# Routing's choice over two iterations, its subtraction on GpSimd, and the fullest expert found in five VectorE operations

## The chip, the cores and the metric

One core of a Trainium2 chip runs the whole kernel as one program. The metric is the device time of one execution in microseconds (us). TensorE (PE) does the matrix products and writes them to PSUM; VectorE (DVE), ScalarE (ACT) and GpSimd (POOL) work on tiles of 128 partitions; SyncE (SP) issues most of the DMAs, and GpSimd issues the indirect ones. Each engine executes its own instructions in order and waits for the others through semaphores.

## The reference

Attention with random features is followed by a mixture of experts with one expert for each token.

```python
h = x @ omega.T - sum(x * x) / 2          # q and k, scaled; batch 8, heads 8, sequence 576, dim 64, features 128
phi = exp(h - max(h)) / sqrt(m)
num = phi(q) @ (phi(k).T @ v);  den = phi(q) @ sum(phi(k)) + 1e-6
x = (num / den) as 4608 tokens x 512
logits = (x / |x|) @ (emb / |emb|).T / tau     # 8 experts
expert_idx = argmax(logits);  gate_w = softmax(logits)[expert_idx]
for e in range(8):
    out[mask_e] = gate_w * (relu(x[mask_e] @ w1[e]) @ w2[e])    # 512 x 1024 x 512
```

## The kernel before

The 4608 tokens are 36 tiles of 128. The first stage is one loop over iterations i from 0 to 42 (END = NTILE + LAG): iteration i projects the keys of tile i and the queries of tile i - 6, and finishes the numerators of tile i - 7. The order of the instructions on all five engines is written out by hand. The order in an iteration is: two projections on TensorE (`proj`, L328, psum tiles pjk and pjq, 64 x 128 x 128 each), the turning of the query features (`qtr`, L404, into nub), maxima on VectorE (`maxima`, L332, tiles nmk and nmq), copies of the turned features (`qcopy`, L409, tile qp, one half on ScalarE and one on VectorE), exponentials on ScalarE (`feats`, L339), the numerators (`num`, L428, into nub), the sums over keys (`kvmm`, L354, kva), and the division on VectorE (`num_out`, L440 to L446), which also leaves each token's eight logits (lg). The psum tile nub is used in turn by L404 and L428, so the next turning waits for the division. After every fifth or ninth tile the sums are closed and turned (L376 to L394), which lengthens that iteration.

Every three tiles make a group (G = 3, groups 0 to 11). The generator `routed(g)` does the routing of a group in steps, and the loop hangs each step on a place in a later iteration, with dictionaries `mid`, `after`, `then` and `ends` that are emptied at fixed points of an iteration (`go`). For a group whose steps begin in iteration b these are:

- step 0, iteration b, at its end: the logits are summed over the heads on GpSimd (L460).
- step 1, iteration b + 1, at `then`: the maximum over the experts (L470) and its subtraction (L471) on VectorE, and three copies of the result into the token rows on GpSimd (L473).
- step 2, iteration b + 1, at `ends`: the first expert that reaches the maximum, in three VectorE operations (L476 to L478, tile sel). From iteration 36 on (group 9 and later) it stands at `mid` of b + 2.
- step 3, iteration b + 2, at `after`: the counting matmuls (L484, L486) that give each token its place among its expert's tokens.
- steps 4 and 5, iteration b + 2, at `ends`: the places on VectorE (L492, L493) and GpSimd (L495, L460), and the first of three casts (L505) and indirect scatters of the rows to DRAM (L507) from GpSimd.
- steps 6 and 7, iterations b + 3 and b + 4, at `ends`: the second and third scatter.

Iteration b + 3 is the b of the next group, and there step 0 of that group is emitted ahead of `go(ends)`. After group 5 (GPICK) `pick_first` finds the fullest expert (L518 to L523) and, one iteration later, `first_known` computes from it (L527 to L532) the addresses (firsti) with which SyncE loads that expert's weights during the loop, and isf and keyc, which are read after the loop. From iteration 28 on these weights are loaded (`first_weights`) and split into two parts each by ScalarE (L545) and GpSimd (L548, and `second_pieces`, L556 and L557, in 16 pieces that the dictionaries `ahead` and `behind` hang on iterations 30 to 41). Iterations 37 to 42 also fill TensorE with the first rows' expert products (`first_steps`, tiles fs_a and fs_o).

The second stage starts at about 235 us: 36 further steps of 128 rows each through an expert's two matrices, in three products each for precision (`products`, L240, psum tiles pa and nu).

## Time and profile before

| | |
|---|---|
| runs of the kernel, us | 638.98, 636.65, 635.66; median 636.65 |
| the profiled execution, us | 639.68 |
| its span from first to last instruction, us | 637.8 |
| mean granted TensorE clock in it | 0.998 of full speed (2.4 GHz) |
| TensorE matmul busy | 620.9 us (97%) |
| VectorE busy | 488.7 us (77%), 953 instructions |
| ScalarE busy | 413.8 us (65%) |
| GpSimd busy | 322.6 us (51%), 420 instructions |

Busy shares are means over stages with different limits. Matmuls are pipelined and their ends are modelled, so a TensorE that is always busy need not be at its peak. The chain of work that ended last is followed back from the last instruction, at each step to what released it; it tells which engine set the pace at each time. "Issue" in it is time in which an engine waited for nothing that the profile shows.

### The profile page before, as it was taken

To read this page: it belongs to the slowest core of one execution; us is meant where nothing else is said; L and a number is where in the kernel's file an instruction comes from. 1 tells how busy PE (TensorE), PEld (TensorE's weight loads), DVE (VectorE), ACT (ScalarE), POOL (GpSimd) and SP (SyncE) were. 2 spreads that over 40 slices of the span, in tenths; PEclk is the share of its full clock that TensorE was granted. 3 is DMA by queue.
4 is the path that set the end of the run, shared out by engine and by line. 5 is a ranking of instruction groups with operands and counts; after the bars stand their busy time and mean duration, and the time that the engine had idled before them with its cause. 6 is when DMAs were issued, how large, how long until landed. Compare 5 with 4: busy or idle time off the path is not lost.

```text
span 637.8 us, 18619 instructions
## 1 busy us (share of the span) xinstructions
PE 620.9 (97%) x6339; PEld 531.7 (83%) x6340; DVE 488.7 (77%) x953; ACT 413.8 (65%) x1071; POOL 322.6 (51%) x420
## 2 busy tenths in 40 slices
PE   8999999999988999999999999999999999999996
PEld 7999999999877787888888888888888888888885
DVE  4799899898778745797688777878777878788652
ACT  5899899889886417664556555656555656565630
POOL 2014333336888744447355646464655555464623
PEclk9999999999999999999999999999999999999999
DMA  7646666668752277878988888898878897979741
GB/s 255 185 153 218 198 209 216 205 226 287 267 194 69 100 251 268 248 203 223 209 238 201 240 208 208 221 234 216 220 203 209 238 231 193 230 218 208 211 117 45
DMA packets 142362, 131.89 MB, mean 207 GB/s; under 512 B 106742, under 2 KB 106870, under 8 KB 142272
## 3 DMA queue, kind: packets, MB, share of 16 engines
q1 hardware_dynamic: 135808, 110.04, 63.8%
q0 software_dynamic: 6320, 20.38, 8.2%
q8 instruction: 57, 0.93, 0.6%
q10 hardware_dynamic: 144, 0.26, 0.2%
q14 instruction: 33, 0.27, 0.1%
HBM read 83.78 MB, written 21.97 MB: 166 GB/s over the span
## 4 chain that ended last, share of the span: by engine, by line
PE 86%; DVE 6%; ACT 3%; issue 3%; DMA 1%; SPq 1%; POOL 0%; POOLq 0%; DVEq 0%; ACTq 0%
PE pa L240 31%; PE nu L240 29%; PE pjk L328 5%; PE nub L428 5%; PE kva L354 5%; PE pjq L328 3%; PE nub L404 2%; PE fs_o L240 2%; ACT ftq L339 1%; ACT ftk L339 1%; PE fs_a L240 1%; DVE qp L409 1%; DVE nmk L332 1%; DVE nmq L332 1%; DMA emb_sb<-emb 1%
## 5 line engine op out<-in xcount | busy, mean ns | idle before, releaser
L240 PE MATMUL nu<-w2h,hh 128*128 (+1 forms) x288 | 112.4, 390 | 0.0
L240 PE MATMUL nu<-w2h,hl 128*128 (+1 forms) x288 | 112.1, 389 | 0.0
L240 PE MATMUL nu<-w2l,hh 128*128 (+1 forms) x288 | 112.0, 389 | 0.0
L240 PE MATMUL pa<-w1h,xh 128*128 (+1 forms) x280 | 109.6, 391 | 0.1
L240 PE MATMUL pa<-w1h,xl 128*128 (+1 forms) x280 | 109.2, 390 | 0.0
L240 PE MATMUL pa<-w1l,xh 128*128 (+1 forms) x280 | 109.0, 389 | 0.0
L953 ACT ACTIVATE pl<-pa 128x512 uint16<-128x512 uint16 x68 | 39.8, 590 | 82.2 <-DMA t<-pl 58.0
L949 DVE TENSOR_REDUCE wd<-t 128x1024 uint16<-128x1024 uint16 (+1 forms) x70 | 90.1, 1292 | 2.2 <-DMA t<-pl 2.1
L339 ACT ACTIVATE ftk<-pjk,nmk 128x128 f32<-128x128 f32 x288 | 85.3, 433 | 5.8 <-DVE nmk L332 5.5
L339 ACT ACTIVATE ftq<-pjq,nmq 128x128 f32<-128x128 f32 x288 | 80.1, 434 | 7.6 <-DVE nmq L332 7.1
L206 POOL TENSOR_TENSOR w1l<-raww,w1h 128x1024 f32 x33 | 80.2, 2432 | 9.3 <-DVE w1h L205 8.3
L949 DVE TENSOR_REDUCE pl<-pa 128x512 uint16<-128x512 uint16 x68 | 46.5, 686 | 47.2 <-ACT pl L953 46.8
L206 POOL TENSOR_TENSOR w2l<-raww,w2h 128x1024 f32 x33 | 79.6, 2411 | 3.8 <-DVE w2h L205 3.8
L328 PE MATMUL pjk<-om,kt 64*128 64x128 f32 x576 | 75.9, 283 | 0.2 <-DVE om L624 0.2
L328 PE MATMUL pjq<-om,qt 64*128 64x128 f32 x576 | 75.6, 283 | 0.3 <-ACT ftk L339 0.2
L993 ACT ACTIVATE hh<-wd 128x1024 fp32r<-128x1024 f32 x33 | 35.0, 1061 | 60.1 <-DVE wd L949 54.2
L328 PEld LDWEIGHTS pjk<-om,kt 64*128 64x128 f32 x576 | 64.5, 188 | 2.8 <-DVE om L624 0.5
L270 POOL DMA_INDIRECT y<-xgp x20 | 22.6, 1132 | 84.2 <-DVE xgp L247 75.6
L328 PEld LDWEIGHTS pjq<-om,qt 64*128 64x128 f32 x576 | 63.9, 188 | 1.2 <-ACT ftk L339 0.7
L240 PEld LDWEIGHTS nu<-w2h,hl 128*128 128x128 f32 x288 | 54.1, 188 | 11.3
L240 PEld LDWEIGHTS nu<-w2h,hh 128*128 128x128 f32 x288 | 54.0, 188 | 11.2 <-issue 0.2
L240 PEld LDWEIGHTS nu<-w2l,hh 128*128 128x128 f32 x288 | 54.0, 188 | 11.2
(313 smaller groups left out, 1262.8 us busy)
## 6 DMA issues: line engine op xcount, KB each, us to landing
raww<-w1q SPq DMA_DIRECT2D x38, 512.0 KB
raww<-w2q SPq DMA_DIRECT2D x38, 512.0 KB
qt<-qT SPq DMA_DIRECT2D x36, 256.0 KB
kt<-kT SPq DMA_DIRECT2D x35, 256.0 KB
xgp<-xs SPq DMA_DIRECT2D x20, 260.5 KB
xg<-xs SPq DMA_DIRECT2D x18, 260.5 KB
rf<-w1q SPq DMA_DIRECT2D x4, 512.0 KB
rf<-w2q SPq DMA_DIRECT2D x4, 512.0 KB
```

The source lines that it names most:

```text
L206: il = nc.gpsimd.tensor_tensor(at(l, dp), raw, at(h, dp).bitcast(F32), op=ALU.subtract)
L240: done.append(nc.tensor.matmul(dst, x[:, c * P : (c + 1) * P], ws.rearrange("p o f -> p (o f)"), start=(begin and i == 0 and k == 0), stop ...
L270: w = nc.gpsimd.indirect_dma_start(out=out, out_offset=bass.IndirectOffsetOnAxis(ap=xg[:, PAY - 1 : PAY].bitcast(I32), axis=0), in_=xg[:, ...
L328: nc.tensor.matmul(st["pj" + w, i, a][:, c, :], st[w, i][r, c, :], om[r, :], start=True, stop=True)
L332: nc.vector.tensor_reduce(nm, st["pj" + which, i, a], axis=AX.X, op=ALU.max, negate=True)
L339: nc.scalar.activation(ft[:, h, :], pj[:, h, :], AF.Exp, bias=nm[:, h : h + 1])
L354: nc.tensor.matmul(acc[c : c + 64, h, :], ft[:, h, c : c + 64], vt[:, 2 * h + a, :], start=begin and h == 0, stop=u == 4 + 4 * b and h == 3,)
L404: nc.tensor.transpose(nu[z][:, j * 64 : j * 64 + 64], st["fq", i, j // 4][r, j % 4, :], ident[r, r])
L428: nc.tensor.matmul(pn[a][z * 64 : z * 64 + 64, h, :], st["qp", i, z][:, 4 * a + h, :], kvs[sb, int(b)][:, h, a * HW : (a + 1) * HW], start ...
L949: nc.vector.tensor_reduce(to, src.unsqueeze(2), axis=AX.X, op=ALU.max)
L953: nc.scalar.activation(planes[1][:, o : o + 512], halved(src)[:, :, 1], AF.Copy)
L993: nc.scalar.activation(hh, wd[:, 0:F], AF.Relu)
```

## The change

Five things change. The subtraction of the maximum goes from VectorE to GpSimd for groups 0 to 6 (GSUB = 7). The last of the three choosing operations (L478) is emitted in the step of the counting matmuls, ahead of them, for groups 0 to 8 (GSEL = 9). The second scatter of a group hangs on a new place, `soon`, in iteration b + 3, which is emptied ahead of step 0 of the next group. The fullest expert is found with a compare and a product in one operation, and the addresses come from one operation over a small table (placei) that GpSimd fills before the loop, in place of five; isf and keyc are computed by three operations of GpSimd in place of two of VectorE, and the tile `first` is gone. One piece of weight splitting in iteration 40 is emitted at `after` and not at the iteration's end.

```diff
 G = 3
 REG = N + P
 GPICK = 5
+GSUB, GSEL = 7, 9
 DUM = E * REG
 ROWS = DUM + P
 RS = 576
...
     isf = const.tile([P, E], F32, name="isf")
     tabi = const.tile([5, NSTEP], I32, name="tabi")
     runi = const.tile([P, E], I32, name="runi")
-    first = const.tile([P, 1], F32, name="first")
     firsti = const.tile([P, NPRE + 2], I32, name="firsti")
     xgp = [const.tile([P, PAY], F32, name=f"xgp{t}") for t in range(NPRE + 1)]
...
                 yield
             mx = new("mx", [P, G])
             nc.vector.tensor_reduce(mx, raw, axis=AX.X, op=ALU.max)
-            nc.vector.tensor_tensor(raw, raw, bc(mx), op=ALU.subtract)
+            (nc.gpsimd if g < GSUB else nc.vector).tensor_tensor(raw, raw, bc(mx), op=ALU.subtract)
             for j in range(G):
                 nc.gpsimd.tensor_copy(st["xr", g * G + j][:, DM : DM + E], raw[:, j])
             yield
             sel = sels[g % 2][:, 0:G]
             nc.vector.scalar_tensor_tensor(sel, raw, 0.0, ibc(iotm), op0=ALU.is_ge, op1=ALU.mult)
             nc.vector.tensor_reduce(mx, sel, axis=AX.X, op=ALU.min)
+            if g < GSEL:
+                yield
             nc.vector.tensor_tensor(sel, ibc(iotm), bc(mx), op=ALU.is_equal)
-            yield
+            if g >= GSEL:
+                yield
             w = 512 - 8 * E
             pr = nu[1][:, w - (G + 1) * E : w].rearrange("p (j e) -> p j e", e=E)
...
             nc.vector.scalar_tensor_tensor(cnt, iote, -float(REG), run, op0=ALU.mult, op1=ALU.add)
             m = small.tile([P, 1], F32, name="m0", tag="m0")
             nc.vector.tensor_reduce(m, cnt, axis=AX.X, op=ALU.max)
-            nc.vector.tensor_scalar(cnt, cnt, m, None, op0=ALU.is_ge)
-            nc.vector.tensor_tensor(cnt, cnt, iotm, op=ALU.mult)
+            nc.vector.scalar_tensor_tensor(cnt, cnt, m, iotm, op0=ALU.is_ge, op1=ALU.mult)
             nc.vector.tensor_reduce(m, cnt, axis=AX.X, op=ALU.min)
             at(ends, st["now"] + 1).append((first_known, m))
         def first_known(m):
-            nc.vector.tensor_scalar(first, m, float(E), None, op0=ALU.add)
-            for t in range(NPRE + 1):
-                nc.vector.tensor_scalar(firsti[:, t : t + 1], first, float(REG), float(t * P), op0=ALU.mult, op1=ALU.add)
-            nc.vector.tensor_copy(firsti[:, NPRE + 1 :], first)
-            nc.vector.tensor_scalar(isf, iote, first, None, op0=ALU.is_equal)
-            nc.vector.scalar_tensor_tensor(keyc, isf, float(2 * E * N), iote, op0=ALU.mult, op1=ALU.subtract)
+            nc.vector.scalar_tensor_tensor(firsti, placei[:, 0], m, placei[:, 1], op0=ALU.mult, op1=ALU.add)
+            nc.gpsimd.tensor_scalar(isf, iotm, m, None, op0=ALU.is_equal)
+            nc.gpsimd.tensor_scalar(keyc, isf, float(2 * E * N), None, op0=ALU.mult)
+            nc.gpsimd.tensor_tensor(keyc, keyc, iote, op=ALU.subtract)
         def first_weights(n):
...
         enbd = once.tile([P, 4, 2, E], F32, name="enbd")
         nc.gpsimd.memset(enbd, 0.0)
         written(nc.sync.dma_start(xs[DUM : DUM + P, 0:PAY], padrow))
+        placei = once.tile([P, 2, NPRE + 2], F32, name="placei")
+        nc.gpsimd.memset(placei[:, 0, 0 : NPRE + 1], float(REG))
+        nc.gpsimd.memset(placei[:, 0, NPRE + 1 :], 1.0)
+        for t in range(NPRE + 1):
+            nc.gpsimd.memset(placei[:, 1, t : t + 1], float(E * REG + t * P))
+        nc.gpsimd.memset(placei[:, 1, NPRE + 1 :], float(E))
         def emb0():
             en2 = once.tile([E, 1], F32, name="en2")
...
         END = NTILE + LAG
-        mid, after, then, ends = {}, {}, {}, {}
+        mid, after, then, soon, ends = {}, {}, {}, {}, {}
         at = lambda d, *key: d.setdefault(key, [])
         for i, f in ((1, emb0), (2, emb1), (4, emb2), (5, emb3)):
             at(ends, i).append((f,))
...
         at(mid, END).append((first_exps,))
         wloads = {w0 + n: n for n in range(2 * NQ - 1)} | {w0 + 8: 2 * NQ - 1}
         second = second_pieces()
-        ahead = {w0 + 7: 2, w0 + 13: 1}
-        behind = {w0 + 2: 2, w0 + 4: 2, w0 + 6: 2, w0 + 8: 2, w0 + 9: 2, w0 + 10: 1, w0 + 11: 1, w0 + 12: 1}
+        ahead = {w0 + 7: 2, w0 + 12: 1, w0 + 13: 1}
+        behind = {w0 + 2: 2, w0 + 4: 2, w0 + 6: 2, w0 + 8: 2, w0 + 9: 2, w0 + 10: 1, w0 + 11: 1}
         for i, n in ahead.items():
             at(after, i).extend([(next, second)] * n)
...
                 at(then, i + 1).append((kv_turned, sb, b))
                 at(then, i + 1).append((kv_logits, sb, b))
                 at(ends, i + 1).append((kv_logits_out, sb, b))
+            go(soon, i)
             if ts and iq % G == 0 and iq < NTILE:
                 steps = routed(iq // G - 1)
                 next(steps)
-                for d, key in ((then if i < NTILE else ends, i + 1), (mid, i + 2) if i >= NTILE else (ends, i + 1), (after, i + 2), (ends, i + 2), (ends, i + 2), (ends, i + 3), (ends, i + 4)):
+                for d, key in ((then if i < NTILE else ends, i + 1), (mid, i + 2) if i >= NTILE else (ends, i + 1), (after, i + 2), (ends, i + 2), (ends, i + 2), (soon, i + 3), (ends, i + 4)):
                     at(d, min(key, END)).append((next, steps, None))
             go(ends, i)
             if NTILE < i <= END:
...
             if n is not None and n % 2 == 0:
                 at(ends, i + 1).append((first_split, n))
         loop.close()
-        assert not any((mid, after, then, ends)), (mid, after, then, ends)
+        assert not any((mid, after, then, soon, ends)), (mid, after, then, soon, ends)
         steps = routed(NTILE // G - 1)
         next(steps)
         next(steps)
```

## Rows read from the trace of the kernel before

**Rows 1.** Page, part 4: the chain that ended last, its share by engine.

```profile
PE 86%; DVE 6%; ACT 3%; issue 3%; DMA 1%; SPq 1%; POOL 0%; POOLq 0%; DVEq 0%; ACTq 0%
```

**Rows 2.** Stretches: start:end and length, busy us of each engine, clock, DMA, GB/s.

```profile
36.50:143.00 106.50, 104.81 (x2453) 99.38 (x2451) 95.49 (x250) 97.51 (x350) 38.88 (x121) 1.00 0.63 204
143.00:182.00 39.00, 35.78 (x834) 33.20 (x832) 33.37 (x81) 36.31 (x125) 29.68 (x69) 1.00 0.80 270
...
235.00:300.00 65.00, 64.67 (x300) 52.93 (x299) 47.02 (x67) 37.73 (x72) 34.20 (x19) 1.00 0.82 244
```

**Rows 3.** Chain in order of time, four hand-overs: start us, us, what.

```profile
55.18 0.30 PE pjk L328
...
57.92 1.17 PE nub L428 x32
...
60.02 0.30 PE pjk L328
...
61.51 0.69 DVE nmk L332
...
62.94 1.22 PE nub L428 x32
64.15 0.03 PE nub L486
...
108.02 0.30 PE pjk L328
...
110.91 1.22 PE nub L428 x32
...
133.19 1.24 PE nub L428 x32
```

**Rows 4.** VectorE in time, group 1: start, us, engine, line, operation, output and inputs.

```profile
58.70 0.17 DVE L470 TENSOR_REDUCE mx<-raw 128x3 f32<-128x24 f32 x1
58.91 0.18 DVE L471 TENSOR_TENSOR raw<-raw,mx 128x24 f32<-128x24 f32 x1
59.01 0.68 DVE L332 TENSOR_REDUCE nmk<-pjk 128x4 f32<-128x512 f32 x1
...
60.77 0.17 DVE L476 SCALAR_TENSOR_TENSOR sel<-raw,iotm 128x24 bf16<-128x24 f32 x1
...
61.19 0.18 DVE L478 TENSOR_TENSOR sel<-iotm,mx 128x24 bf16<-128x24 f32 x1
...
62.71 0.68 DVE L332 TENSOR_REDUCE nmq<-pjq 128x4 f32<-128x512 f32 x1
```

**Rows 5.** VectorE in time around pick_first and first_known.

```profile
130.83 0.17 DVE L518 SCALAR_TENSOR_TENSOR cnt<-iote,run 128x8 f32<-128x8 f32 x1
...
131.77 0.68 DVE L332 TENSOR_REDUCE nmk<-pjk 128x4 f32<-128x512 f32 x1
...
135.92 0.14 DVE L527 TENSOR_SCALAR first<-m 128x1 f32<-128x1 f32 x1
...
136.78 0.68 DVE L332 TENSOR_REDUCE nmk<-pjk 128x4 f32<-128x512 f32 x1
```

**Rows 6.** Line 495: duration in ns, least, median, most; first and last start.

```profile
L495 POOL TENSOR_TENSOR base<-base,sel x11: 224/225/232, 51.0 to 212.7; 128x24 f32<-128x24 f32 x11
```

**Rows 7.** GpSimd in time around the sums of group 10.

```profile
205.39 0.24 POOL L460 TENSOR_TENSOR raw<-lg 128x24 f32<-128x24 f32 x1
205.57 0.18 POOL L505 CAST posi<-pos 128x1 int32<-128x1 f32 x1
...
207.16 0.41 POOL L556 CAST w2h<-rf 128x256 fp32r<-128x256 f32 x1
```

**Rows 8.** VectorE in time, groups 8 and 10; in brackets its idle time before.

```profile
176.68 0.40 DVE L478 TENSOR_TENSOR sel<-iotm,mx 128x24 bf16<-128x24 f32 x1
...
206.33 0.17 DVE L470 TENSOR_REDUCE mx<-raw 128x3 f32<-128x24 f32 x1
...
207.51 0.69 DVE L409 COPY qp<-nub 128x512 f32<-128x512 f32 x1 [0.16 <-PE nub L404]
```

## The prediction

> **What bounds the kernel now.** I read the chain that ended last first, then the stretches, then the neighbourhood of the lines that the change touches. Over the whole span the chain is TensorE for 86%, VectorE for 6%, ScalarE for 3% [rows 1]. The stretches say where those other shares lie [rows 2]. From 235 us on, in the expert stage, TensorE is busy 64.67 of 65.00 us, and nothing that the change touches runs there, so all it can do is start that stage sooner or later. The attention loop is different: from 36.5 to 143 us three engines are nearly full together (TensorE 104.81, ScalarE 97.51, VectorE 95.49 of 106.50 us), and from 143 to 182 us GpSimd joins with 29.68 of 39.00 us. TensorE paces an iteration, but VectorE has so little room that a few tenths more on it in one iteration arrive at TensorE.
>
> How they arrive is seen at a hand-over [rows 3]: the iteration's first projection starts, VectorE takes the negated maxima (nmk) and copies the transposed features (qp), and the numerator matmuls (nub L428) wait for that copy. Undisturbed, projection to numerator takes 57.92 - 55.18 = 2.74 us. In the iteration behind a group's choice it takes 62.94 - 60.02 = 2.92 us, and the last of the three hand-overs of this kind (groups 1, 2 and 4 of 0 to 11) 110.91 - 108.02 = 2.89 us. The cause stands in VectorE's rows [rows 4]: its last choosing operation (sel, L478) starts at 61.19, only then comes nmk at 61.51 [rows 3]. So a late hand-over costs about 0.18 us, though VectorE spends five small operations on the group. The rest is hidden.
>
> **Part by part.** *The subtraction of groups 0 to 6 goes to GpSimd.* The maximum starts at 58.70, the subtraction at 58.91, the next maxima at 59.01 [rows 4]: without the dependent pair VectorE is freed of 0.10 to 0.21 us per group. On GpSimd a two-input operation of this shape takes 225 ns [rows 6]. The wait that is added is that of sel (L476) on GpSimd; behind it on VectorE are the next nmk and qp. But sel starts at 60.77, 1.9 us after the maximum's end, so 0.23 us and two semaphores fit. If GpSimd were busy then, the whole excess would fall on nmk; for these groups the heavy weight splitting has not begun.
>
> *The last choosing operation of groups 0 to 8 moves into the next iteration*, between the two maxima nmq that start at 62.71 [rows 4]. It takes 0.18 us from one iteration and puts 0.10 to 0.18 into the next. TensorE gains a wait: the counting matmuls (L484, L486) now need an operation of the same iteration; queued behind them are the kv sums and the next projection. The counting matmuls run at 64.15 [rows 3], the operation would end near 62.71 + 0.60 + 0.18 = 63.5, so 0.65 us of cover. Without it the delay would go straight to TensorE.
>
> Together, at the three late hand-overs: VectorE is relieved by 0.3 to 0.4 us, more than the 0.18 that shows, and TensorE's own order is late next. I take 0.18 x 3 = 0.54 us, between 0 (something else holds nub) and 3 x 0.31 = 0.93.
>
> *The fullest expert (group 5).* Five operations take from 130.83 to 131.77, 0.94 us; four remain, so a fifth, 0.19 us, goes. They are on the chain: the numerator follows at 133.19 behind nmk and qp [rows 3, 5]. With the subtraction (0.20) and the moved operation (0.11 net) VectorE loses 0.50 us there; TensorE's own pace may hold part. I take 0.40, between 0.2 and 0.5. One iteration later seven operations take 136.78 - 135.92 = 0.86 us [rows 5] and one of some 0.2 us remains, with three on GpSimd that nobody needs before the loop's end. VectorE gets 0.66 us, TensorE what a late hand-over is worth: 0.2, between 0 and 0.66.
>
> *Group 8's moved operation* took 0.40 us instead of 0.18, while GpSimd was splitting weights [rows 4, 8]; it stands in front of nmk there. In its new place it meets the splitting too. I take 0.1, between -0.2 and +0.4.
>
> The Trainium skill, "SBUF — State Buffer", section "Who interferes with whom", says that VectorE operations with two SBUF inputs and GpSimd operations that read SBUF exclude each other for a whole instruction. The 0.40 us of this operation agrees. By that rule its new place could cost up to one of GpSimd's instructions, and group 8's term would be nearer its lower end.
>
> *A scatter is issued ahead of the next group's sums, not behind them.* On GpSimd's queue everything counts: the index cast at 205.57 and its scatter hold the queue until the next piece at 207.16 [rows 7], 1.59 us. For early groups GpSimd idles before the sums, and this is hidden. For group 10 it does not idle. Its sums end at 205.39 + 0.24 = 205.63; behind the scatter they end at 207.22. VectorE's maximum starts at 206.33 [rows 8], so VectorE would wait 0.9 us, with the copy qp (207.51, which has 0.16 us of idle before it) queued behind it and the numerator behind that. I take 0.90 - 0.16 = 0.75 us lost, between 0 (GpSimd is ahead by then) and 0.9. Group 7 meets the same order with most of the delay covered: 0.1, between 0 and 0.7 (the delay and its moved operation beside weight splitting). The last scatters of each group leave no later, and the moved piece of weight splitting in iteration 40 shifts GpSimd's work without adding any; no one waits for it before the loop's end: 0. The six fills of the small table run before the loop, with GpSimd idle for long after: 0.
>
> **The sum.** Gains 0.54 + 0.40 + 0.20 + 0.10 = 1.24 us, losses 0.75 + 0.10 = 0.85, net -0.39. The profiled execution took 639.68 us (span 637.8), so its like would be 639.29. That execution is 3.03 us above the median of the runs, 636.65; the difference carries over: 636.3 us.
>
> **The rivals.** *The whole gain is kept.* For: GpSimd also starts sooner when VectorE does, and its order before group 10 may leave room. Against: in the rows the cast follows the sums without idle time [rows 7]. Then -1.24: 635.4.
>
> *GpSimd's queue becomes the bound, slower than before.* The scatter ahead of the sums holds VectorE's maximum in groups 7 and 10, while the hand-overs gain nothing because TensorE paces them. It decides as soon as the sums of group 10 end after VectorE is free: +0.85 to +1.6, about 637.7. For: the 1.59 us. Against: the 2.92 us at hand-overs, which only VectorE explains.
>
> *The work only moves.* What leaves one iteration lands in the next, and the relief does not reach TensorE: groups gain nothing, the shortened choice of the fullest expert keeps 0.2, the losses are half: 636.9. The Trainium skill, "Perfetto Trace Analysis", section "Optimizing Scalar/DVE Operations", says that moving work between VectorE and GpSimd might not help, since they share a port; that would bring this case. In the rows GpSimd would run beside nmk, and no run here shows that pair slowed.
>
> *Another phase of the whole loop*, by over 3 us either way: nothing in the rows points there.
>
> **How the numbers follow.** Forecast 0.42, whole gain 0.25, GpSimd's queue 0.18, work only moves 0.10, another phase 0.05. The single bounds add to 0.93 + 0.5 + 0.66 + 0.4 = 2.49 us of gain without losses, 634.2, and to 1.6 us of loss (0.9 + 0.7) plus 0.2 for group 8, with a gain of 0.2, 638.25. The three runs of before lie from 1 us below to 2.3 us above their median; half a microsecond of that beyond either bound gives 633.8 to 638.7. A measurement of this kernel can tell about 0.5%, 3.2 us, from no change. All mechanisms but the last stay inside it: same 0.90. Faster by more (under 633.5) needs all gains at their upper ends or another phase, 0.06; slower by more (over 639.8) another phase or both queue losses in full with more behind them, 0.04.
>
> **What would show it.** Right: the hand-overs of groups 1, 2 and 4 at 2.74 us; VectorE's pair at group 5 shorter by 0.2 and 0.66 us; GpSimd's subtraction done well before sel; VectorE idle before the maximum of group 10, with GpSimd's sums named. Wrong: hand-overs still at 2.9 us, a wait of the counting matmuls for sel, VectorE idle in sel's place, or a shift that begins behind 235 us, which none of the steps explains.

## The result, and the profile after

The change makes the kernel slower. The changed kernel's median is 641.23 us (639.20 to 643.00, 6 runs), beside 636.29 us (635.66 to 638.98, 6 runs) for the kernel before: ratio 1.0064 [1.0036, 1.0093]. Two further comparisons, each beside its own runs of the kernel before, give 1.0035 [1.0018, 1.0052] and 1.0050 [1.0034, 1.0066], so some 2 to 4 us. The forecast was 636.3 us, between 633.8 and 638.7.

The profiled execution of the changed kernel took 639.2 us (span 637.6), as long as the shortest of its six; that of the kernel before took 639.68 us, longer than all of its six. **The two traces are equally long and can't show the loss by their lengths.** It has to be read from single waits, from iterations, and from kernels that carry one part of the change.

The chain that ended last, by engine (page of the changed kernel, part 4), answers to [rows 1]:

```profile
PE 83%; DVE 6%; DMA 4%; POOL 3%; issue 3%; ACT 1%; POOLq 0%; SPq 0%; DVEq 0%; ACTq 0%
PE pa L240 31%; PE nu L240 29%; PE pjk L328 5%; PE kva L354 4%; PE nub L428 4%; PE pjq L328 3%; DMA qt<-qT 3%; PE nub L404 2%; PE fs_o L240 2%; DVE nmq L332 1%; DVE nmk L332 1%; PE fs_a L240 1%; DVE xr L443 1%; DVE qp L409 1%; POOL xs L510 1%
```

DMA and GpSimd have grown from 1% and 0% to 4% and 3%, and two names are new: the query load (qt<-qT) and the indirect scatter (xs, L510). The same stretches as in [rows 2] (start:end, length, busy us of TensorE's matmuls, its weight loads, VectorE, ScalarE and GpSimd, clock, DMA share, GB/s):

```profile
36.50:143.00 106.50, 104.83 (x2449) 99.33 (x2448) 93.14 (x235) 96.61 (x350) 41.25 (x132) 1.00 0.65 205
143.00:182.00 39.00, 35.23 (x832) 32.74 (x832) 33.08 (x82) 36.16 (x125) 29.40 (x68) 1.00 0.81 272
235.00:300.00 65.00, 64.65 (x299) 52.90 (x299) 47.14 (x68) 38.29 (x73) 34.67 (x18) 1.00 0.81 247
```

VectorE lost 2.35 us of work in the first stretch (95.49 to 93.14), and the expert stage is as full as before (64.65 of 65.00). TensorE's waits (what waited, line, releaser: us in total, times, longest), the first four rows of the changed kernel:

```profile
PE pjq L328 <- DMA qt<-qT: 2.6, 3, 1.5
PE nub L404 <- DVE run L496: 2.5, 3, 1.5
PE nub L428 <- DVE qp L409: 1.8, 4, 0.7
PE warm L627 <- POOL one L72: 1.3, 1, 1.3
```

and the first two rows of the kernel before:

```profile
PE nub L428 <- DVE qp L409: 3.3, 6, 0.8
PE nub L404 <- DVE run L493: 2.1, 2, 1.2
```

The late copies have become fewer, as predicted. A new row stands on top: three times the projection of the queries waited for its load. The first of the three, in order of time. GpSimd's scatter, changed kernel (start, us, engine, line; in brackets the idle time before):

```profile
54.56 0.99 POOL L510 DMA_INDIRECT xs<-xr,posi  x1 [0.28 <-POOL posi L508]
55.56 0.77 POOL L460 TENSOR_TENSOR lg<-lg 128x96 f32<-128x96 f32 x2
```

SyncE's queue (value load, then query load):

```profile
54.72 0.33 SPq L312 DMA_DIRECT2D vt14v<-v  x1
55.14 2.02 SPq L318 DMA_DIRECT2D qt<-qT  x1
```

The chain of waits (start, us, what):

```profile
55.14 5.17 DMA qt<-qT
60.31 0.14 issue
60.45 0.34 PE pjq L328
```

TensorE's own row:

```profile
60.45 0.34 PE L328 MATMUL pjq<-om,qt 64*128 64x128 f32 x1 [0.43 <-DMA qt<-qT]
```

The same scatter in the kernel before:

```profile
57.54 1.01 POOL L507 DMA_INDIRECT xs<-xr,posi  x1 [0.39 <-POOL posi L505]
```

The second scatter now starts some 3 us earlier, ahead of the query load by half a microsecond instead of behind it. The load takes 5.17 us to land; TensorE needs it about 4.4 us after its issue: the projection starts at 59.53 with the keys, and the queries follow 0.92 us later, at 60.45 (the 0.43 in the row is what two matmuls of the keys leave of it). Among the 12 of this kernel's 36 query loads that have a landing record, landing took 3.0 us at least, 4.3 in the middle, 6.3 at most: a load with 4.4 us between issue and use has hardly any slack. In the kernel before it has no more (issued at 55.63, projection at 59.95, without a wait); its trace has no landing record of a query load.

**Iterations as a ruler.** On VectorE every iteration from 7 to 42 starts one `rr` (L440); an iteration's length is the time from the start of the `rr` before it to that of its own. In the changed kernel:

```profile
58.88 0.16 DVE L440 TENSOR_SCALAR rr<-nub 128x8 f32<-128x8 f32 x1
...
64.61 0.16 DVE L440 TENSOR_SCALAR rr<-nub 128x8 f32<-128x8 f32 x1
```

gives 5.73 us for iteration 14, the one with the late load; the kernel before takes 4.89. The device time less the start of the last `rr` is 424.42 us before (639.68 - 215.26), 424.31 after, and 424.34 and 424.42 in two kernels below (soon_back, qfirst_only): what differs between these four traces differs in the loop. It isn't so in every trace: soon_only below, a 644.09-us execution and the longest of its twelve, has 428.24, so part of its length lies behind the loop. A trace is one execution, and its length is not the kernel's.

### The profile page after: what moved, and what is told of

Read it like the earlier page. It is cut to its first block, busy times and chain, and to the rows that moved or that the text cites. A ratio compares the mean times of both kernels' runs of the same rounds, so it can differ in the third digit from the quotient of the medians.

```text
span 637.6 us, 18621 instructions
## 1 busy us (share of the span) xinstructions
PE 620.1 (97%) x6339; PEld 531.8 (83%) x6340; DVE 488.1 (77%) x939; ACT 412.8 (65%) x1071; POOL 324.0 (51%) x436
## 4 chain that ended last, share of the span: by engine, by line
PE 83%; DVE 6%; DMA 4%; POOL 3%; issue 3%; ACT 1%; POOLq 0%; SPq 0%; DVEq 0%; ACTq 0%
PE pa L240 31%; PE nu L240 29%; PE pjk L328 5%; PE kva L354 4%; PE nub L428 4%; PE pjq L328 3%; DMA qt<-qT 3%; PE nub L404 2%; PE fs_o L240 2%; DVE nmq L332 1%; DVE nmk L332 1%; PE fs_a L240 1%; DVE xr L443 1%; DVE qp L409 1%; POOL xs L510 1%
## 5 line engine op out<-in xcount | busy, mean ns | idle before, releaser
L332 DVE TENSOR_REDUCE nmk<-pjk 128x4 f32<-128x512 f32 x72 | 48.8, 686 | 21.1 <-PE pjk L328 19.9
```

The lines of the kernel that those rows point to most:

```text
L332: nc.vector.tensor_reduce(nm, st["pj" + which, i, a], axis=AX.X, op=ALU.max, negate=True)
```

## The experiments

Kernels of a group ran on one chip, beside runs of the kernel before on that chip. From group to group the kernel before differs by more than the kernels do (medians 637.51, 640.39, 636.71, 636.34 and 639.62 us), by 2.1 us even between A and E, both on chip 3, so only ratios within a group are compared. A ratio stands with its 95% interval; it is not the quotient of the two medians (after_third's would be 1.0038).

| group | kernel | median us | ratio to the kernel before |
|---|---|---|---|
| A | after_again | 639.90 | 1.0035 [1.0018, 1.0052] |
| A | soon_back | 637.59 | 1.0006 [0.9990, 1.0023] |
| A | soon_only | 640.27 | 1.0036 [1.0019, 1.0053] |
| A | choice_only | 637.73 | 1.0005 [0.9993, 1.0017] |
| B | first_only | 639.42 | 0.9989 [0.9975, 1.0004] |
| B | after_qfirst | 640.52 | 1.0002 [0.9984, 1.0019] |
| B | back_qfirst | 638.66 | 0.9979 [0.9969, 0.9990] |
| C | after_third | 639.13 | 1.0050 [1.0034, 1.0066] |
| C | after_qfirst_same | 637.01 | 1.0009 [0.9995, 1.0022] |
| C | soon_early | 639.34 | 1.0044 [1.0023, 1.0065] |
| C | soon_late | 638.53 | 1.0038 [1.0026, 1.0049] |
| D | qfirst_only | 635.21 | 0.9981 [0.9966, 0.9996] |
| D | back_qfirst_same | 636.02 | 0.9998 [0.9980, 1.0015] |
| D | dummy_small | 637.13 | 1.0009 [0.9992, 1.0026] |
| D | dummy_full | 637.69 | 1.0019 [1.0003, 1.0036] |
| E | sel7_qfirst | 638.20 | 0.9975 [0.9960, 0.9989] |
| E | first_qfirst | 639.12 | 1.0001 [0.9980, 1.0022] |

### Which part of the change costs the time (group A)

The changed kernel as it is (after_again), the changed kernel with the second scatter at its old place (soon_back), the kernel before with only the scatter moved (soon_only), and with only the choice changed, GSUB and GSEL (choice_only).

```diff
# soon_back, against the changed kernel; soon_only makes the reverse edit in the kernel before
-                for d, key in (..., (ends, i + 2), (soon, i + 3), (ends, i + 4)):
+                for d, key in (..., (ends, i + 2), (ends, i + 3), (ends, i + 4)):
# choice_only, against the kernel before
-            nc.vector.tensor_tensor(raw, raw, bc(mx), op=ALU.subtract)
+            (nc.gpsimd if g < GSUB else nc.vector).tensor_tensor(raw, raw, bc(mx), op=ALU.subtract)
...
+            if g < GSEL:
+                yield
             nc.vector.tensor_tensor(sel, ibc(iotm), bc(mx), op=ALU.is_equal)
```

> The changed kernel as it is, for a second profile and for the scale of the other three. All theories expect 640 to 642 us beside 636.3 us of before (its six runs so far). The profiled execution so far, 639.2 us, was the fastest of its six; there TensorE waited 2.6 us for the query loads (qt), three times, each time for a load that SyncE issued just as GpSimd issued the second scatter of a group. Theory S (the earlier scatter makes the query loads late) expects that a slower execution shows more such waits, 4 to 7 us together. Theory V (the relieved loop itself runs up to its loads) expects waits for loads too, but spread over all iterations, not only over those with the moved scatter. Theory A (the tiles moved in memory) expects no wait for a load but single operations that take longer.

> The changed kernel with the second scatter of a group put back to the end of its iteration, all else as changed. Theory S: the loss goes, 635.0 to 636.5 us, no waits for qt, the stall of VectorE before the maximum of group 10 gone too. Theory V: the loads still pace the loop, 640 to 641 us. Theory A: 640 to 641 us.

> The kernel before with nothing changed but the place of the second scatter: ahead of the next group's sums. Theory S: 639 to 642 us, TensorE waits for qt behind loads issued beside the scatter. Theory V: as before, 636 to 637 us, since nothing is taken from VectorE. Theory A: as before, 636 to 637 us.

> The kernel before with only routing's choice changed: the subtraction of groups 0 to 6 on GpSimd, the last choosing operation of groups 0 to 8 beside the counting matmuls. Theory S: 635.3 to 636.5 us, the hand-overs of groups 1, 2 and 4 at 2.74 us and not 2.9. Theory V: 638 to 641 us, with TensorE waiting for loads although the scatter is where it was. Theory A: as S.

The scatter's place alone makes the kernel before slower by as much as the whole change (1.0036 and 1.0035), and putting it back removes the loss (1.0006). The other parts move nothing that the interval shows. The wait for the query load appears in soon_only at the same place as in the changed kernel:

```profile
61.24 0.34 PE L328 MATMUL pjq<-om,qt 64*128 64x128 f32 x1 [0.85 <-DMA qt<-qT]
```

Iteration 14 takes 5.73, 5.72 and 5.78 us in the changed kernel, after_again and soon_only, and 4.89 to 4.94 in the kernel before, choice_only and soon_back. In soon_back the load is issued at 55.50 and the projection starts at 59.91 without a wait.

Not all came as theory S had it. after_again's trace, of an execution no slower than the first (638.78 us), has 1.3 us of such waits, in iterations 14 and 35; the slower one with 4 to 7 us was not met. soon_back took 637.59 us, above the 635.0 to 636.5 expected, and one wait for a query load is left in it, 0.78 us in iteration 35.

### Is it the query load? (groups B and C)

If the scatter harms by delaying the query load, then issuing that load earlier takes the harm away with the scatter left where it is. SyncE issues it ahead of the value load: the query load starts at 55.14 us in the changed kernel and at 52.88 in group B's trace, the value load at 54.72 and 55.12.

```diff
-        def load(i):
+        def load(i, q=-1):
...
                 loadk(i, nc.sync)
+            loadq(q)
+            if i < NTILE:
                 loadv(i)
...
-                load(i + (4 if i < 2 else 2))
+                load(i + (4 if i < 2 else 2), iq + 2 if i > LAG - 1 else -1)
...
-            loadq(iq + 2 if i > LAG - 1 else -1)
```

back_qfirst is the same edit in soon_back, first_only is the kernel before with the fullest expert found in five operations, and before_again the kernel before once more (one run, 638.63 us).

> The kernel before once more, for a second profile: the one shown belongs to an execution of 639.68 us, 2 us above the median of the runs since (637.5). Theory S (the scatter ahead of the sums makes query loads late) expects no wait of TensorE for a query load in the first 143 us, and an iteration 14 (from its division on VectorE to that of the next) of 4.9 us, where the two kernels with the early scatter show 5.7 to 5.8. Theory V (the relieved loop runs up to its loads) expects the same here, as nothing is relieved. If the first profile was only an odd execution, its iterations 16 and 34 (6.95 and 7.29 us) come out at about 6.2 and 6.6.

> The kernel before with only the fullest expert found in five operations of VectorE (and three of GpSimd). Prediction's step: 0.2 to 1.1 us faster, 636.5 to 637.3 beside 637.5 us; iterations 27 and 28 shorter by 0.2 each. A rival: the small gain is used up between 143 and 182 us, where ScalarE and GpSimd pace the loop, and the time stays at 637.5 us though the two iterations are shorter.

> The changed kernel, scatter ahead of the sums as changed, but SyncE issues each query load ahead of the value load and not behind it, so that it no longer waits for the end of the sums over keys: about 2 us earlier. If the lateness of the query load is how the scatter costs time (theory S), the time falls from 639.9 to 636.5 to 638 us, and TensorE has no wait for qt. If the scatter costs time in another way (GpSimd's queue, VectorE waiting before the maximum of group 10), it stays at 639 to 640 us with the waits for qt gone.

> The changed kernel with the second scatter back at the end of its iteration and the query load issued ahead of the value load. Theory S: no worse than with the scatter back alone (637.6 us), and better by the few remaining waits for qt there, 0.3 to 0.8 us: 636.5 to 637.5 us, the fastest of all.

before_again has no wait of TensorE for a query load and an iteration 14 of 4.89 us, as theory S expected. Its iteration 16 is back at 6.22 us, but iteration 34 takes 7.30 as in the first profile. first_only shows its two iterations shorter by 0.2 us each; 0.9989 [0.9975, 1.0004] doesn't tell its total from the kernel before.

Group C repeats it beside the unchanged pair on one chip, and splits the scatter by groups of tokens: `(soon if i < 24 else ends, i + 3)` moves it for groups 0 to 4 only (soon_early), the reverse for groups 5 to 10 only (soon_late).

> The changed kernel as it is, for the comparison on one chip with the three that follow (chips differ: the kernel before took 637.5 us on one and 640.4 us on another). All theories: 1.003 to 1.006 of the kernel before.

> The changed kernel with each query load issued ahead of the value load, beside the changed kernel itself on the same chip. Lateness of the query load as the whole cost of the early scatter: 0.997 to 0.998 of the changed kernel, at or under the kernel before. If GpSimd's queue (the sums of groups 7 and 10 behind the scatter) costs as much as its rows say, 1.0 us of 2.2 stays: 1.001 of the kernel before. If the load does not matter: the time of the changed kernel.

> The changed kernel with the second scatter ahead of the sums for groups 0 to 4 only, at the iteration's end for the others. Query loads as the cause: a wait of TensorE for qt of 0.4 to 1.5 us in iteration 14 or 23, iterations 31 and 41 as without the early scatter (5.5 and 4.7 to 5.0 us), 1.001 to 1.002 of before. GpSimd's queue as the cause: the time of the kernel before, since GpSimd idles before the sums of these groups.

> The changed kernel with the second scatter ahead of the sums for groups 5 to 10 only. GpSimd's queue as the cause: iterations 31 and 41 at 5.7 to 5.8 and 5.5 us, 0.3 and 0.6 to 0.8 us longer than without the early scatter, 1.001 to 1.003 of before, iterations 14 and 23 at 4.9 us. Query loads as the whole cause: at most the wait in iteration 35 is left, 1.000 to 1.001 of before.

On one chip the earlier load takes the changed kernel from 639.13 to 637.01 us (1.0050 to 1.0009). SyncE's rows of after_qfirst:

```profile
52.88 0.38 SPq L320 DMA_DIRECT2D qt<-qT  x1
55.12 0.33 SPq L314 DMA_DIRECT2D vt14v<-v  x1
```

and iteration 14 takes 4.78 and 4.93 us with it. These 2.1 us are not all the scatter's: the same order also takes 1.1 us off the kernel before (636.34 to 635.21, group D). What the scatter costs with the query load first is seen beside the kernel that differs by the scatter's place alone: 640.52 against 638.66 us in group B (1.0002 and 0.9979), and 1.0009 against 0.9998 between groups C and D. So 0.7 to 1.9 us of its cost stay, and the totals don't say how much goes through the query load.

The traces say where. TensorE's idle time before projections of queries, single waits of over 0.15 us, added over the iterations from 8 on, one execution each:

| kernel | early scatter | query load | idle, us (iterations) |
|---|---|---|---|
| changed kernel | yes | second | 2.63 (14, 23, 35) |
| after_again | yes | second | 1.29 (14, 35) |
| after_third | yes | second | 1.61 (15, 35) |
| soon_only | yes | second | 2.72 (14, 23, 35) |
| soon_early | groups 0 to 4 | second | 3.45 (15, 32, 35) |
| soon_late | groups 5 to 10 | second | 1.37 (15, 32, 35) |
| before, before_again, first_only | no | second | 0 |
| choice_only | no | second | 0.30 (33) |
| soon_back | no | second | 0.78 (35) |
| dummy_small (group D) | one added, groups 0 to 4 | second | 1.21 (15, 33, 35) |
| dummy_full (group D) | one added, groups 0 to 4 | second | 1.70 (14, 23, 33, 35) |
| after_qfirst | yes | first | 0.92 (35) |
| after_qfirst_same | yes | first | 1.57 (35) |
| qfirst_only, back_qfirst, back_qfirst_same, sel7_qfirst, first_qfirst | no | first | 0 |

For some of these waits the profile names an operation of VectorE or ScalarE that ended just before. Where the load has a landing record, as in iterations 23 and 35 of soon_only and 35 of after_again, the projection starts 0.13 to 0.14 us behind the landing, as in the changed kernel's first wait; where it has none, that the wait is the load's is concluded from the place. With the earlier load no trace has the waits in iterations 14, 15 and 23. It leaves the one in iteration 35, and beside it the wait of VectorE in iteration 41 that is told of below; that iteration takes 5.47 and 5.63 us in after_qfirst and after_qfirst_same, 4.88 and 4.54 in back_qfirst and back_qfirst_same.

```profile
173.69 0.34 PE L330 MATMUL pjq<-om,qt 64*128 64x128 f32 x1 [1.57 <-DMA qt<-qT]
```

So the early scatter makes query loads late, and that is a large part of the loss; the exact share is open. The split by groups did not come out: the halves were expected at 1.000 to 1.003, and each costs nearly what the whole costs (1.0044 and 1.0038 beside 1.0050). In soon_early iterations 14 and 23 take 5.19 and 4.94 us, nearly as without the scatter, and its longest waits stand in iterations 32 and 35, where its scatter is at the old place. The parts don't add, and why is open.

### Does the load matter without the scatter, and is it the scatter's data? (group D)

qfirst_only is the kernel before with the query load first. The two dummies are soon_back with one more scatter at the new place for groups 0 to 4, into rows that nobody reads, 16 or 512 columns wide:

```diff
+            nc.gpsimd.indirect_dma_start(
+                out=xd, out_offset=bass.IndirectOffsetOnAxis(ap=ids[:, g : g + 1], axis=0),
+                in_=st["xr", g * G + 1][:, 0:512], in_offset=None, bounds_check=5 * P - 1, oob_is_err=False,
+            )
...
+                if i < 24:
+                    at(soon, i + 3).append((dummy, iq // G - 1))
```

> The kernel before with nothing changed but SyncE's order: each query load ahead of the value load. If query loads are late in the kernel before as well, 0.9970 to 0.9985 of it; if they are late only beside the moved scatter, 0.9995 to 1.0005.

> The changed kernel with the second scatter back at the iteration's end and query loads ahead of value loads, on the chip of the other three. If the query loads explain what the choice and the fullest expert could not show: 0.997 to 0.998 of before, and 0.0005 to 0.002 below query loads first alone. If the relief of VectorE is worth nothing in time: the same as query loads first alone.

> The changed kernel with the second scatter back at the iteration's end, and for groups 0 to 4 an additional scatter of 16 columns (64 bytes a row) to rows that nobody reads, ahead of the next group's sums. If the data that a scatter moves beside the query load is the cause: 0.999 to 1.002 of before, as without it. If its issue or its 128 rows of whatever size are the cause: 1.003 to 1.005, like the early scatter of groups 0 to 4 (1.0044).

> The same with 512 columns (2048 bytes a row), about what the true scatter moves. Data as the cause: 1.003 to 1.006 of before, with waits of TensorE for qt in iterations 12 to 25. Issue as the cause: the same time as with 16 columns. If neither matters, and what costs is only that the true rows are written earlier: both at 1.000 to 1.002.

Issued first, the query load gives 0.9981 [0.9966, 0.9996], the shortest time of all these kernels on its chip and what was expected if it is late in the kernel before as well. The two traces of that kernel show no wait for it, so where the 0.2% come from is not shown. back_qfirst_same took 636.02 us and not less than qfirst_only, which group E looks into. The dummies came out at 1.0009 and 1.0019, under the 1.003 that either the data or the issue was to cost, and under soon_early's 1.0044: by the totals neither is shown, and they fit the third case, that only the earlier writing of the true rows costs. One iteration of the traces differs: with 512 columns iteration 14 takes 6.38 us, with 16 columns 4.92, as without any. GpSimd's added scatter in dummy_full, and TensorE's row for the late projection:

```profile
53.84 1.00 POOL L519 DMA_INDIRECT xd<-xr,ids  x1 [0.16 <-issue]
```

```profile
60.60 0.34 PE L328 MATMUL pjq<-om,qt 64*128 64x128 f32 x1 [1.08 <-ACT ftk L339]
```

The releaser named, the last exponential of the keys, ended at 60.52, but the projection doesn't need it: in dummy_small it starts at 59.88, ahead of these exponentials. The load has no landing record in that trace; that the 1.08 us are the load's is concluded from the place. GpSimd spent the same time on the narrow scatter (0.99 us at 54.67), which speaks for the data. It is one iteration of one execution each, and such waits change place between executions, so it is not shown. The Trainium skill, "DMA: Bandwidth & Descriptors", section "Queues, rings and completion order", says that each DMA engine serves the queues that have work for it in turn, packet by packet; by that a scatter on GpSimd's queue slows a load on SyncE's, and this pair agrees as far as one iteration goes. No run here shows the order of the packets.

### Where did the predicted gain go? (group E)

qfirst_only and back_qfirst_same differ by the choice and the pick alone, ran on one chip, and neither trace has a late load. Lengths in us, added over iterations:

| iterations | qfirst_only | back_qfirst_same |
|---|---|---|
| 9 to 26 (choice of groups 0 to 4) | 93.91 | 93.95 |
| 27 (group 5, pick_first) | 5.51 | 5.30 |
| 28 (first_known) | 5.90 | 5.70 |
| 31 and 32 (groups 6 and 7, weight splitting) | 10.51 | 11.10 |
| 29 to 42 | 71.43 | 72.17 |

The pick wins 0.41 us. The choice wins nothing, and in iteration 32, where VectorE has no idle time, it loses: the moved operation of group 7 takes 0.78 us instead of 0.18. VectorE of back_qfirst_same and, in its old place, of qfirst_only:

```profile
157.76 0.78 DVE L482 TENSOR_TENSOR sel<-iotm,mx 128x24 bf16<-128x24 f32 x1
```

```profile
156.00 0.18 DVE L480 TENSOR_TENSOR sel<-iotm,mx 128x24 bf16<-128x24 f32 x1
```

At that moment GpSimd works through a block of weight splitting (back_qfirst_same):

```profile
157.76 2.78 POOL L550 TENSOR_TENSOR w1l<-rf,w1h 128x256 fp32r<-128x256 f32 x4
```

sel7_qfirst leaves this operation in its old place for groups 7 and 8 (`GSUB, GSEL = 7, 7`); first_qfirst is qfirst_only with the pick, and nothing of the choice.

> The changed kernel with the second scatter at its old place, the query load ahead of the value load, and the last choosing operation moved for groups 0 to 6 only (GSEL = 7, was 9). Theory (the moved operations of groups 7 and 8 meet GpSimd's weight splitting in their new place and give back what the five-operation pick wins): VectorE's iteration 32 falls from 5.61 us to 4.8 to 4.9, the moved operation of group 7 from 0.78 us to 0.2 to 0.3 in its old place; the loop's end (last start of rr) comes 0.4 to 0.7 us sooner than with GSEL = 9, near 210.1; time 0.9975 to 0.999 of the kernel before. Rival (iteration 32 is bound by something else, and the operation only fills VectorE's idle time): iteration 32 stays at 5.5 or more, ratio 0.9990 to 1.0005.

> The kernel before with the query load ahead of the value load and the fullest expert found in five operations, nothing of the choice moved. Theory (the pick's two gains reach the loop's end if nothing gives them back): iterations 27 and 28 at 5.30 and 5.70 us, against 5.51 and 5.90 with the query load alone, the loop's end 0.4 us sooner than the 209.97 of that kernel, ratio 0.997 to 0.9985. Rival (a later iteration of the loop gives them back whatever the choice does): iterations 29 to 42 together longer than 71.43 us by about 0.4, ratio 0.998 to 0.9995, as with the query load alone.

In sel7_qfirst the operation is back at 0.18 us and iteration 32 falls from 5.61 to 5.14 us, not to the 4.8 expected: the operation ahead of it, sel (L478), took 0.62 us there and 0.27 in qfirst_only.

```profile
157.18 0.62 DVE L478 SCALAR_TENSOR_TENSOR sel<-raw,iotm 128x24 bf16<-128x24 f32 x1
157.83 0.18 DVE L479 TENSOR_REDUCE mx<-sel 128x3 f32<-128x24 bf16 x1
158.05 0.18 DVE L482 TENSOR_TENSOR sel<-iotm,mx 128x24 bf16<-128x24 f32 x1
```

So the moved operation made 0.47 of the 0.84 us that this iteration lost; sel's 0.35 us more is nearly the rest, and probably the same meeting at another operation. The ratio, 0.9975 [0.9960, 0.9989], is the lowest of all, but back_qfirst, which differs by GSEL alone, had 0.9979 and 0.9998 on two chips, so the total doesn't confirm the 0.5 us. The loop's end was no help, since this chip's traces carry more of the odd waits told of below (last `rr` at 213.12 us, 210.1 expected). first_qfirst shows the pick's two gains at their places (5.31 and 5.70 us), and yet 1.0001 [0.9980, 1.0022] in total and its last `rr` at 213.19: neither theory's total came, and 0.4 us can't be told in it.

## Why the prediction was wrong, point by point

**The step that failed** is *A scatter is issued ahead of the next group's sums*. It counted the scatter on GpSimd's queue, "For early groups GpSimd idles before the sums, and this is hidden", and did not ask what the scatter's transfer meets. It meets query loads that have hardly any slack, the first of them issued half a microsecond later. Where 0.85 us were taken for the whole step, the scatter's place costs 2.3 us (after_again and soon_back, 639.90 and 637.59) and 2.8 us (soon_only, 640.27 against 637.51): TensorE waits 1.3 to 2.7 us for late query loads in the four traces of these kernels with the whole scatter early, and 0 in both of the kernel before. These waits stood in no sum and no rival. The rival *GpSimd's queue becomes the bound* had the right edit and half of the cause: its wait of VectorE for group 10's sums came, but it did not know of the loads. Its price, +0.85 to +1.6, is neither shown nor excluded by the 0.7 to 1.9 us that stay with the query load first, since the late load of iteration 35 is in them too.

**Behind the early scatter, group 10: right at the place, the size open.** VectorE waits for GpSimd's sums where the prediction said, 0.84 us against 0.9:

```profile
206.93 0.18 DVE L470 TENSOR_REDUCE mx<-raw 128x3 f32<-128x24 f32 x1 [0.84 <-POOL raw L460]
```

Iteration 41 takes 5.58, 5.52, 5.42 and 5.51 us with the scatter ahead (changed kernel, after_again, after_third, soon_late) and 4.99 and 4.92 without (soon_back, soon_early): 0.4 to 0.6 us, where 0.75 was taken. (For groups 9 and 10 the maximum stands at the end of iteration b + 1, behind that iteration's `rr`, so the wait falls into the next length.) Against the kernel before nothing is lost there: its iteration 41 takes 5.39 us without the scatter ahead, and soon_only's 4.98 with it, though VectorE waits 0.76 us in that too. So 0.4 to 0.6 us is the term beside the other parts of the change, and what makes iteration 41 long in the kernel before is open. *Group 7* was taken at 0.1. Iteration 31 takes 5.76 to 5.82 us with the scatter ahead and 5.48 without, in kernels that have the other parts, but iteration 32 gives it back: both together take 10.96 us in the changed kernel and 11.09 in soon_back (11.48 in after_third). So this term is not seen.

**The late hand-overs: right at two places of three, nothing in the sum.** In soon_back the projection behind the choice of group 1 starts at 59.97 and the numerator at 62.62, of group 4 at 106.89 and 109.53: 2.65 and 2.64 us where [rows 3] gave 2.92 and 2.89. The gain there is 0.25 and not 0.18. Group 2's falls by 0.1 only (2.94 to 2.84 us by the starts of TensorE's rows). But the next iteration is longer by as much: iterations 25 and 26 go from 6.21 and 4.77 us to 6.00 and 5.00 (qfirst_only, back_qfirst_same), 13 and 14 from 5.09 and 4.68 to 4.89 and 4.93. So the 0.54 us were 0. This is the rival *The work only moves*. In iteration 14 the relief turns into idle time of VectorE, which waits for the projection (back_qfirst_same; in qfirst_only it comes without a wait):

```profile
60.78 0.69 DVE L334 TENSOR_REDUCE nmk<-pjk 128x4 f32<-128x512 f32 x1 [0.29 <-PE pjk L330]
```

TensorE stands idle in iterations 13 and 14 of neither kernel, so there it holds the pace, as the prediction feared ("TensorE's own order is late next"). In iteration 26 VectorE has no such wait, and the moved operation takes 0.2 us of its time there.

**Group 5 and first_known: half, and right.** The pick gives 0.21 and not 0.40: choice_only has 5.51 us in iteration 27 like the kernel before, first_only 5.31, so the moved subtraction and operation add nothing. The changed kernel's rows of VectorE show the four operations in place of five (0.73 us from 130.94 to 131.67, 0.94 in [rows 5]):

```profile
130.94 0.17 DVE L521 SCALAR_TENSOR_TENSOR cnt<-iote,run 128x8 f32<-128x8 f32 x1
131.14 0.16 DVE L523 TENSOR_REDUCE m<-cnt 128x1 f32<-128x8 f32 x1
131.33 0.23 DVE L524 SCALAR_TENSOR_TENSOR cnt<-cnt,m,iotm 128x8 f32<-128x8 f32 x1
131.59 0.16 DVE L525 TENSOR_REDUCE m<-cnt 128x1 f32<-128x8 f32 x1
131.67 0.68 DVE L332 TENSOR_REDUCE nmk<-pjk 128x4 f32<-128x512 f32 x1
```

first_known was taken at 0.20 and gives 0.20 (5.90 to 5.70 us). There TensorE is late next, as the step feared: VectorE now idles 0.34 us for its projection.

```profile
136.39 0.69 DVE L332 TENSOR_REDUCE nmk<-pjk 128x4 f32<-128x512 f32 x1 [0.34 <-PE pjk L328]
```

**The moved operation beside weight splitting** was taken as a gain of 0.1 for group 8. It takes 0.65 us in the changed kernel and 0.50 in soon_back, 0.40 before [rows 8], and group 7's, 0.78, is dearer still. Iterations 31 and 32 together lose 0.59 us beside qfirst_only, of which sel7_qfirst gives back 0.47 in iteration 32. The section "Who interferes with whom" of the Trainium skill's "SBUF — State Buffer" says that a VectorE instruction with two SBUF inputs contends with a GpSimd instruction that reads SBUF. The trace agrees: group 7's operation is 0.60 us longer than alone, less than the 0.73 us that one of GpSimd's splitting instructions takes. The prediction had that end in its bounds for groups 7 and 8 but in the sum for neither.

**GpSimd's subtraction** was hidden, as said: 0.23 us, done before sel needs it.

```profile
58.45 0.23 POOL L471 TENSOR_TENSOR raw<-raw,mx 128x24 f32<-128x24 f32 x1 [1.80 <-DVE mx L470]
```

**The sum again**, an estimate from these rows: gains 0.21 + 0.20, losses 0.59 (moved operations), so +0.2 us without the early scatter, 1.0003; soon_back measured 1.0006. With it, iterations 8 to 42 together are longer than in soon_back by 3.1, 1.3 and 2.1 us in the three traces of the changed kernel. Of that, iterations with a late query load (14, 15, 23, 35) make 3.0, 1.1 and 0.8, and iteration 41 makes 0.6, 0.5 and 0.4; the rest is scattered, of either sign. That gives +1.5 to +3.3 us, where the three comparisons gave ratios of 1.0035 to 1.0064, some 2 to 4 us. The range failed since it was made of the terms that had been listed; nothing in it stood for a resource that no step had looked at. (By its own working its lower end is 633.7 and not 633.8, which changes nothing.)

## What to carry to other kernels

When a DMA is moved, set it against every load that is issued near its new place, and compare that load's time from issue to use with the landing times in the profile, not only against the queue of the engine that issues it. A load whose slack is smaller than the spread of its landing times is worth trying earlier whatever else changes: here that alone gave 0.2%, more than all the work taken off VectorE, though the traces don't show by which wait. And when a repair is tried, compare with the kernel that has the repair without the fault, not only with the one that has neither. An operation moved from one iteration into the next gains nothing where another engine holds the pace over both, and it can cost four times as much beside another engine's block of work.

## What the runs showed that was not expected

- Query loads of 256 KB took 3.0 to 6.3 us to land in one execution, and waits for them change place between executions: iteration 23 takes 6.01 us in the changed kernel and 4.93 in after_again and after_third.
- The longest such wait, in iteration 35, doesn't need this group's scatter ahead, and issuing the load first doesn't remove it. The load issued at about 169.5 us, when large weight loads run, held TensorE for 1.50 us in the changed kernel, and for 2.05 us in soon_early, where this group's scatter is at its old place. Yet all eight traces with early scatters have it (0.80 to 2.05 us), and of the twelve without only soon_back and the two dummies (0.29 to 0.78). What links them is open. soon_early:

```profile
176.07 0.34 PE L328 MATMUL pjq<-om,qt 64*128 64x128 f32 x1 [2.05 <-DMA qt<-qT]
```

- In many executions, of either kernel, one or two of the iterations 15, 16, 24 and 25 are longer by about 0.7 us than in others. For iteration 15 of after_third, soon_early, soon_late and dummy_small the profile names a late query load. For the others it doesn't: iteration 16 takes 6.95 us in the kernel before and 6.22 in before_again, whose iteration 25 takes 6.93 instead of 6.22. There the cause is open.
- A two-input VectorE operation on 128 x 24 elements takes 0.17 or 0.18 us alone and up to 0.78 us beside GpSimd's weight splitting.
